# Attention, expert layers and cosine layer on one core: another start for head 0's scores

## The chip, the core and the metric

The kernel runs on one core of a Trainium2 chip. The metric is the device time of one execution in microseconds (us). The kernel before took 740.85 us, the median of three runs (740.27 to 741.19). The profile was taken from one execution of its own, which took 739.14 us; the program's span in that trace is 737.6 us.

The names used here: PE is TensorE (matmuls and transposes), ACT is ScalarE, DVE is VectorE, POOL is GpSimd, SP is SyncE, which issues nearly all DMAs. SBUF is the working memory, PSUM the eight banks into which PE writes.

## The reference

Three layers in a row. Only the first is touched by the change:

```python
q_pool = q.reshape(B, H, S // 2, 2, D).mean(axis=3)      # B=2, H=8, S=1152, D=64
scores = scale * np.matmul(q_pool, k.transpose(0, 1, 3, 2))
attn = softmax(scores)
x = np.matmul(attn, v)          # -> 1152 tokens of 512 columns
x = moe(x)                      # 8 experts, the 2 best of each token
out = (h * np.cos(h)) @ w_out   # h = x @ w_in
```

Neighbouring rows of q are averaged, so each head and batch has 576 pooled rows against 1152 keys.

## The kernel before, in words

Every fp32 operand of a matmul is split in two: a high part, rounded to the format that PE reads (fp32r), and a low part, the rest. A score is q times k in three or four such products. For scores, high and low part of k stand on top of each other in one tile: head_dim is 64, so 64 partitions hold the high part and 64 the low part (`kt`), and the high part of q stands twice (`q2`). One matmul with `q2` then gives high times high plus high times low; a second with the low part of q (`l2`) adds the rest.

Heads go in pairs (hp = 0 to 3), and in a pair there are head hl = 0 and hl = 1. Of each head there are nine tiles of 128 query rows: tiles 0 to 3 lie in batch 0, tile 4 lies in both, tiles 5 to 8 in batch 1. That makes 72 steps, one a tile, and each engine's instructions stand in the order in which the program is written. Step n does, in this order on PE: the scores of tile n+1 (three parts of 384 keys, `s_bank`, L310), between the second and the third of them the first of three groups of transposes of tile n's exponentials (`t_pe`, L348), then the other two groups, and among these 6 or 9 matmuls of attention times v of earlier tiles (L386). DVE takes the maximum of each score part (L324, L326). ACT copies the transposes out (L361, L369), and it does three exponentials with their sums (`s_exp`, L333). POOL splits every third transposed group (L371, L372) and, as single long pieces, v, k and q of heads to come.

PSUM: scores take turns in four banks (`s`), transposes in three (`pt`), attention times v has one (`pa`). A new tile takes the bank that was released longest ago, and PE waits until its last reader is done. With four banks and three score parts a step, the first part of a step's scores needs the exponential of a step earlier, the second part that of part 0 of the tile before, the third that of part 1.

Before the first step stands a prologue (L774 to L862). There head pair 0 is loaded and prepared: q of both heads in two halves (batch 0 first, L206), k of batch 0 in six small pieces (L108), k of batch 1 (L102). DVE adds the q pairs (L211), PE transposes q (`q_front`, L219) and k of both heads together (`k_direct`, L189; ACT L194 takes the high part out of PSUM, DVE L195 the low part), and tile 0's scores start. The rest of pair 0 (batch 1 of q; k of batch 1: `k_group` L180, split on POOL, `k_split`) is prepared between tile 0 and the first steps, with copies on DVE (L845, L847) and ACT (L849) in steps 1 and 2. Ten bf16 matmuls that compute nothing (`warm`, L419) keep PE busy until q is there. A table (`plan`) says in which step the loads, splits and transposes of later heads come.

Of the kernel before, what the change touches and what calls it, by code (L numbers as in the profile page):

```python
# [22 lines left out]
def attn_moe_cos_kernel(ctx, tc, q, k, v, w_gate, w_noise, noise, w1, w2, w_in, w_out, out):  # L23
# [159 lines left out]
    KW = (12, 3, 3, 3)  # L183
    WQ = 10

    def k_direct(hp, b, j, kk, bank):
        p = bank()
        for i in range(3):
            nc.tensor.transpose(p[:, i * 128:(i + 1) * 128], KN[hp, b][:, 3 * j + i].rearrange("p h d -> p (h d)"), ident)  # L189
        cs = slice(384 * j, 384 * (j + 1))  # L190
        for hl, t in enumerate(kk):
            me, ot = slice(hl * 64, hl * 64 + 64), slice(64 - hl * 64, 128 - hl * 64)
            yield
            nc.scalar.activation(t[me, cs], p[me, 0:384], AF.Copy)  # L194
# [20 lines left out]
    def q_front(j, b):  # L215
        QB[j] = p = tbank()
        rs = slice(b * 64, b * 64 + 64)
        for i in range(3):
            nc.tensor.transpose(p[:, i * 64:(i + 1) * 64], QP[0][rs, 3 * j + i].rearrange("p h d -> p (h d)"), ident[rs, rs])  # L219

    def q_part(t, b, j):
        return t[:, b * QB1:b * QB1 + SQ].rearrange("p (s c) -> p s c", c=9)[:, :, 3 * j:3 * j + 3]

    def q_hi(b, j, o):
        nc.scalar.activation(q_part(o, b, j), QB[j][:, 0:192].rearrange("p (i s) -> p s i", i=3), AF.Copy, scale=1.0 / 16.0)

    def q_lo(b, j):
        nc.vector.scalar_tensor_tensor(q_part(QL[0], b, j), QB[j][:, 0:192].rearrange("p (i s) -> p s i", i=3), 1.0 / 16.0,
                                       q_part(QS[0].bitcast(F32), b, j), op0=OP.mult, op1=OP.subtract)
# [498 lines left out]
    def plan():  # L728
# [5 lines left out]
        for hp in range(HP):  # L734
            n0 = 18 * hp
            for hl in range(2):
                for b in range(B):
                    s = n0 + 9 * hl + 5 * b
                    at(s - 7, load_v, hp, hl, b)
                    at(s - 3, split_v, hp, hl, b)  # L740
            if hp:
# [7 lines left out]
                at(m + 2, load_k, hp, 0)  # L749
                for j in range(3):  # L750
                    at(m + (3 + 2 * d, 5 + d, 6 + d)[j], q_group, hp, j)
# [13 lines left out]
                at(n0 + 1, q_bd, hp, 1)  # L765
        at(8, load_gate)
# [4 lines left out]
    pres = ExitStack()  # L771
    pro = pres.enter_context(tc.tile_pool(name="pro", bufs=1, side="right", reuse_waits="tile"))
    load_qb(0, 0)
    load_qb(1, 0)  # L774
    load_k(0, 0)
    load_k(0, 1, pro)
    load_qb(0, 1)
    load_qb(1, 1)
    warm(tbank, WQ)
    QP[0] = prep.tile([128, 9, 2, 64], F32, name="qp", bufs=1)  # L780
    QH = QS[0] = prep.tile([128, 1216], F32R, name="sh", bufs=2)
    QL[0] = prep.tile([128, 1216], F32R, name="ql", bufs=1)
    t = t0 = Q2[0, 0] = qk.tile([128, 1216], F32R, name="q2", bufs=3)
    L0 = QL2[0, 0] = qk.tile([128, 1216], F32R, name="l2", bufs=2)
    for i in range(3):
        z = slice(512 * i, min(512 * i + 512, 1216))
        nc.gpsimd.tensor_scalar(L0[64:128, z], ZERO[64:128, 0:z.stop - z.start], 1.0, 0.0, op0=OP.mult, op1=OP.add)
    for hl in range(2):
        pool_qb(hl, 0, nc.vector)
    for j in range(3):  # L790
        q_front(j, 0)
    kk = k_tiles(0, 0)
    kbank = [lambda: ps.tile([128, 512], F32, name="s", bufs=4)] * 2 + [lambda: ps.tile([128, 512], F32, name="pa", bufs=1)]
    kg = [k_direct(0, 0, j, kk, kbank[j]) for j in range(3)]
    for g in kg:
        next(g)
    for j in range(3):
        q_hi(0, j, QH)
        q_lo(0, j)
    c = slice(0, SQ)  # L800
    nc.scalar.activation(t[64:128, c], QH[0:64, c], AF.Copy)
    nc.vector.tensor_scalar(t[0:64, c], QH[0:64, c], 1.0, 0.0, op0=OP.mult, op1=OP.add)
    nc.gpsimd.tensor_scalar(L0[0:64, c], QL[0].bitcast(F32)[0:64, c], 1.0, 0.0, op0=OP.mult, op1=OP.add)
    for g in kg:
        next(g)
    next(kg[0])
    s_mm(0)
    QR = pro.tile([128, 1216], F32, name="qr")
    z = slice(SQ, QB1)
    nc.gpsimd.memset(QR[:, z], 0.0)  # L810
    nc.gpsimd.tensor_scalar(QH[:, z], QR[:, z], 1.0, 0.0, op0=OP.mult, op1=OP.add)
    for hl in range(2):
        pool_qb(hl, 1, nc.gpsimd)
    QN.clear()
# [4 lines left out]
    load_q(1, 0)  # L819
    load_q(1, 1)  # L820
    for i in range(3):
        s_max(0, i)
    for g in kg[1:]:
        next(g)
    KN.pop((0, 0))
    for j in range(3):
        k_group(0, 1, j)
# [3 lines left out]
    for i in range(3):  # L831
        s_bank(1, i)
        if i == 0:
            for j in range(3):
                q_front(j, 1)
    for i in range(3):
        s_max(1, i)
    for j in range(3):
        q_hi(1, j, QR)
        q_hi(1, j, QH)  # L840
    k_split(0, 1)
    c = slice(SQ, 1216)
    nc.gpsimd.tensor_tensor(QL[0][:, c], QR[:, c], QH.bitcast(F32)[:, c], op=OP.subtract)
    lo0 = QL[0].bitcast(F32)
    ev.setdefault(1, []).insert(0, (lambda: nc.vector.tensor_scalar(  # L845
        t0[0:64, c], QH[0:64, c], 1.0, 0.0, op0=OP.mult, op1=OP.add), ()))
    ev.setdefault(2, []).insert(0, (lambda: nc.vector.tensor_scalar(  # L847
        L0[0:64, c], lo0[0:64, c], 1.0, 0.0, op0=OP.mult, op1=OP.add), ()))
    ev.setdefault(2, []).insert(0, (lambda: nc.scalar.activation(t0[64:128, c], QH[0:64, c], AF.Copy), ()))  # L849
    k_asm_a(0, 1)  # L850
    q_asm(0, 1, False)
    l_asm(0, 1)
    for n in sorted(e for e in ev if e < 0):
        for f, a in ev[n]:
            if f != load_v:
                f(*a)
    pres.close()
    kbp.append(qes.enter_context(tc.tile_pool(name="kbp", bufs=1, reuse_waits="tile")))
    k_stack(0)
    k_asm_b(0, 1)  # L860
    nc.sync.dma_start(KB[0, 1].bitcast(F32)[0:64], KT[0, 1, 0].bitcast(F32)[64:128])
    q_bd(0, 1)  # L862
# [17 lines left out]
    for n in range(NTOT - 1):  # L880
        hp, hl, t = tiles[n]
        for f, a in ev.get(n, []):
            if f not in (q_group, k_group):
# [44 lines left out]
        t_lo(n, 1)  # L928
        if xg:
# [12 lines left out]
        fl = [(f, a) for f, a in ev.get(n, []) if f in (q_group, k_group)]  # L942
# [770 lines left out]
```

## Time and profile before

| what | value |
|---|---|
| median of three runs | 740.85 us (740.27 to 741.19) |
| the profiled execution | 739.14 us |
| its span | 737.6 us |
| PE busy | 722.5 us, 98% of the span |
| DVE, ACT, POOL busy | 562.3, 528.8, 301.9 us |
| PE on the chain that ended last | 90% |

The page's table of 40 slices shows each slice of 18.4 us in tenths of busy time: PE reads 6 in the first slice, 9 in all others but the last. PEclk is the granted TensorE clock in tenths of full speed.

A row of the timeline reads: start in us, duration in us, engine, line of the kernel, operation, out<-in, partitions x elements and type, how many instructions are merged (x3), and in brackets the engine's idle time ahead of it and what ended it. A duration of merged rows is that of the whole group. Instructions of one engine overlap a little, so three in a row take less than three times one.

### The profile page before, as it was taken

How to read it: one execution, taken by the hardware profiler on the slowest of the kernel's cores; microseconds unless marked ns; L12 is line 12 of the kernel's file. 1: busy time of each engine (PE TensorE's matmuls, PEld its weight loads, DVE VectorE, ACT ScalarE, POOL GpSimd, SP SyncE). 2: the span in 40 equal slices, each digit the busy share in tenths (PEclk: the TensorE clock that was granted, in tenths of full speed). 3: DMA queues.
4: the chain of work that ended last, by engine and by line, in shares of the span. 5: the costliest groups of instructions: out<-in, count | busy, mean ns of one | idle time of the engine just before them, and what ended most of it. 6: DMA issues, size and time to landing. Idle time of an engine off the chain costs nothing.

```text
span 737.6 us, 13760 instructions
## 1 busy us (share of the span) xinstructions
PE 722.5 (98%) x4803; PEld 673.9 (91%) x4803; DVE 562.3 (76%) x1161; ACT 528.8 (72%) x1200; POOL 301.9 (41%) x329
## 2 busy tenths in 40 slices
PE   6999999999999999999999999999999999999997
PEld 4899999999999989999999999999889989888885
DVE  5888788888878988879889887776677776556562
ACT  5999799979988964458777676766588665555443
POOL 5988867877977973212022021103187110000000
PEclk9999999999999999999999999999999999999999
DMA  9957756695665511798999999968353210010001
GB/s 207 244 94 183 184 130 147 163 237 106 161 140 146 179 44 29 248 314 295 363 371 328 334 345 330 329 233 286 119 171 97 85 29 1 1 44 0 1 1 60
DMA packets 75329, 125.02 MB, mean 169 GB/s; under 512 B 11950, under 2 KB 42030, under 8 KB 75254
## 3 DMA queue, kind: packets, MB, share of 16 engines
q1 hardware_dynamic: 68678, 101.92, 47.3%
q0 software_dynamic: 5568, 19.14, 7.4%
q10 hardware_dynamic: 1008, 3.02, 1.6%
q8 instruction: 40, 0.66, 0.4%
q14 instruction: 35, 0.29, 0.1%
HBM read 82.15 MB, written 20.33 MB: 139 GB/s over the span
## 4 chain that ended last, share of the span: by engine, by line
PE 90%; DVE 4%; ACT 3%; DMA 1%; issue 0%; SPq 0%; ACTq 0%; DVEq 0%
PE h L1145 20%; PE acc L1145 16%; PE acc L1177 11%; PE s L310 10%; PE pa L386 9%; PE pt L348 9%; PE t L1145 7%; PE pt L694 2%; PE t L1137 1%; PE pt L984 1%; PE t L1194 1%; PE pt L180 1%; DMA raw<-in_moe_w_dram 1%; DVE nm L324 1%; DVE el L365 1%; DMA qn<-in_q_dram 1%
## 5 line engine op out<-in xcount | busy, mean ns | idle before, releaser
L324 DVE TENSOR_REDUCE nm<-s 128x1 f32<-128x384 f32 x216 | 112.1, 551 | 23.4 <-PE s L310 21.8
L333 ACT ACTIVATE p<-s,nm 128x384 f32<-128x384 f32 x216 | 125.1, 583 | 2.8 <-DVE nm L326 1.5
L1145 PE MATMUL h<-xe,u 128*128 128x320 f32 (+5 forms) x768 | 120.1, 306 | 0.0
L1145 PEld LDWEIGHTS h<-xe,u 128*128 128x128 f32 x768 | 109.6, 188 | 0.5
L642 DVE TENSOR_TENSOR u<-raw,u 128x1024 fp32r<-128x1024 f32 x66 | 80.9, 1227 | 34.4 <-ACT u L641 33.6
L348 PE MATMUL pt<-ident,p 128*128 128x128 f32 x645 | 105.0, 272 | 0.0
L310 PE MATMUL s<-kt,q 128*128 128x384 f32 x240 | 88.8, 386 | 3.7 <-DVE kt L195 2.1
L348 PEld LDWEIGHTS pt<-ident,p 128*128 128x128 f32 x645 | 81.7, 140 | 5.7
L386 PE MATMUL pa<-eh,v 128*128 128x320 f32 (+1 forms) x279 | 86.5, 324 | 0.0
L641 ACT ACTIVATE u<-raw 128x1024 fp32r<-128x1024 f32 x73 | 77.1, 1057 | 10.3 <-DMA raw<-in_moe_w_dram 5.8
L361 ACT ACTIVATE eh<-pt 128x384 fp32r<-128x384 f32 x144 | 68.9, 501 | 20.3 <-PE pt L348 19.0
L386 PE MATMUL pa<-el,v 128*128 128x320 f32 (+1 forms) x279 | 82.4, 309 | 0.0
L372 POOL TENSOR_TENSOR el<-rw,eh 128x384 fp32r<-128x384 f32 x71 | 71.9, 1012 | 5.9
L365 DVE TENSOR_TENSOR el<-pt,eh 128x384 fp32r<-128x384 f32 x144 | 72.9, 547 | 1.0 <-ACT eh L361 0.9
L1177 PE MATMUL acc<-hh,u 128*128 128x320 f32 (+5 forms) x448 | 71.8, 302 | 0.1
L1145 PE MATMUL acc<-u,gh 128*128 128x512 f32 x216 | 66.9, 391 | 0.0
L310 PE MATMUL s<-kt,l 128*128 128x384 f32 x198 | 66.3, 337 | 0.0
L1177 PEld LDWEIGHTS acc<-hh,u 128*128 128x128 f32 x448 | 64.7, 188 | 0.4 <-ACT hh L1156 0.4
L1232 POOL DMA_DIRECT2D w_d<-dw x16 | 9.0, 563 | 130.5 <-DVE dw L1231 130.5
L371 POOL TENSOR_SCALAR eh<-rw 128x384 fp32r<-128x384 f32 x71 | 36.8, 518 | 42.0 <-ACT rw L369 39.7
L386 PEld LDWEIGHTS pa<-el,v 128*128 128x128 f32 x279 | 52.9, 190 | 0.0
L386 PEld LDWEIGHTS pa<-eh,v 128*128 128x128 f32 x279 | 52.8, 189 | 0.0
(292 smaller groups left out, 1605.9 us busy)
## 6 DMA issues: line engine op xcount, KB each, us to landing
raw<-in_moe_w_dram SPq DMA_DIRECT2D x64, 512.0 KB
raw<-in_moe_w_in_dram SPq DMA_DIRECT2D x16, 512.0 KB
raw<-in_moe_w_out_dram SPq DMA_DIRECT2D x16, 512.0 KB
w_d<-dw POOLq DMA_DIRECT2D x16, 512.0 KB, 5.4
raw<-w_d SPq DMA_DIRECT2D x13, 512.0 KB
vn<-in_v_dram SPq DMA_DIRECT2D x16, 288.0 KB
q<-sh SPq DMA_DIRECT2D x14, 304.0 KB
l<-ql SPq DMA_DIRECT2D x14, 304.0 KB
```

Source lines behind the costliest of these rows:

```text
L310: nc.tensor.matmul(o, l, r, start=(m == 0), stop=(m == len(mm) - 1))
L324: nc.vector.tensor_reduce(NM[n][:, i:i + 1], SB[n][i][:, 0:384], axis=AX.X, op=OP.max, negate=True)
L333: nc.scalar.activation(P[n][i], SB[n][i][:, 0:384], AF.Exp, bias=NM[n][:, 3:4], accum_out=SUMS[:, t, 2 * hp + hl, i:i + 1])
L348: nc.tensor.transpose(p[:, c], P[n][j][:, c], ident)
L361: nc.scalar.activation(t_dst(n, j)[0], t_src(n, j), AF.Copy)
L365: nc.vector.tensor_tensor(el, t_src(n, j), ef, op=OP.subtract)
L372: nc.gpsimd.tensor_tensor(el, rw, ef, op=OP.subtract)
L386: nc.tensor.matmul(st["p"][:, 0:w], V2[hp, hl, b][:, VC[c] if hp + b else c, :], (EH, EL)[s][:, c, EB[g]:EB[g] + w], start=(c == 0 and s = ...
L641: nc.scalar.activation(b[:, 0], r, AF.Copy)
L642: st_w["lo"].tensor_tensor(b[:, 1], r, b.bitcast(F32)[:, 0], op=OP.subtract)
L1145: nc.tensor.matmul(o, l, r, start=first and i == 0, stop=last and i == len(seq) - 1)
L1177: nc.tensor.matmul(ACC[e, d][:, 0:CAPS[e]], w[:, i, 128 * d:128 * d + 128], r[:, 0:CAPS[e]], start=f == 0 and r is hh and i == 0, stop=f = ...
```

## The change

Only the start is changed, and the handling of head pair 0.

- Loads: q and k of head 0 alone, batch 0 first, in four whole DMAs (`load_h0`); then two loads of v, then q of head 1 (`load_h1`). k of head 1 (`load_k1`) follows once head 0's k has been transposed.
- q of head 0: DVE adds the pairs in two pieces (6 and 3 of 9 groups, `pool_p`), ACT writes each sum a second time beside it, so that one transpose gives both copies of q. ACT takes the high part and DVE the low part out of PSUM straight into `q2` and `l2` (`q0_hi`, `q0_lo`). Batch 1 is added on POOL and goes the same way after tile 0's maxima.
- k of head 0: batch 0 is transposed alone (`k0_tr`, 64 columns each) and split by ACT and DVE (`k0_part`); batch 1 by `k0b_copy` (three copies on ACT) and `k0b_split` (POOL and four DMAs).
- Head 1 is prepared inside the steps: its k in steps 1 to 3 (`k_group`, 3 transposes and one ACT copy each, split on POOL in step 4, eight DMAs in step 6), its q in steps 4 to 6 (`q1_group`: 3 transposes, two ACT copies; the low parts on DVE a step later, `late`). These groups take their PSUM bank from the four of the scores (`gbank`).
- One q group of head pair 1 moves from step 6 to step 7, one split of v from step 2 to step 5, one load of k from step 2 to step 4. The idle matmuls are eleven and read a tile of ones, which is set first on DVE.

```diff
@@ functions of the prologue @@
+    XS0 = X.rearrange("p t d -> p (t d)")[:, 1920:1920 + S]
     def k_group(hp, b, j):
...
-        p = tbank()
+        p = tbank() if hp else gbank()
...
+    PART = (slice(0, 6), slice(6, 9))
+    def pool_p(hl, rs, cs, eng):
+        t = QN[0, hl][rs].rearrange("p (s r) d -> p s r d", r=2)
+        o = QP[0, hl][rs, cs]
+        eng.tensor_tensor(o[:, :, 0, :], t[:, cs, 0, :], t[:, cs, 1, :], op=OP.add)
+        if eng is nc.vector:
+            nc.scalar.activation(o[:, :, 1, :], o[:, :, 0, :], AF.Copy)
+        else:
+            eng.tensor_scalar(o[:, :, 1, :], o[:, :, 0, :], 1.0, 0.0, op0=OP.mult, op1=OP.add)
+    def gbank():
+        return ps.tile([128, 512], F32, name="s", bufs=4)
...
+    def q1_group(j):
+        cs = slice(3 * j, 3 * j + 3)
+        q_tr(1, slice(0, 128), cs, ("h", j))
+        src = QB["h", j][:, 0:384].rearrange("p (i b s) -> p b s i", i=3, b=2)
+        for b in range(2):
+            nc.scalar.activation(q0_out(Q2[0, 1], b, cs), src[:, b], AF.Copy, scale=1.0 / 16.0)
+        late.append(lambda: [nc.vector.scalar_tensor_tensor(q0_out(QL2[0, 1], b, cs), src[:, b], 1.0 / 16.0,
...
+    def k0_tr(j, p):
         for i in range(3):
...
+            nc.tensor.transpose(p[LO, i * 128:(i + 1) * 128], KN[0, 0][:, 0, c:c + 64], ident)
+    def k0_part(j, p):
+        kt, c = KT[0, 0, 0], slice(384 * j, 384 * j + 384)
+        nc.scalar.activation(kt[LO, c], p[LO, 0:384], AF.Copy)
+        nc.vector.tensor_tensor(kt[HI, c], p[LO, 0:384], kt.bitcast(F32)[LO, c], op=OP.subtract)
+    def k0b_copy():
...
+        k_tr(1, 0, pa)
+        nc.scalar.activation(t[:, 0:384], pa[:, 0:384], AF.Copy)
+        k_tr(1, 1, pb)
+        nc.scalar.activation(t[:, 384:512], pb[:, 0:128], AF.Copy)
+        nc.scalar.activation(t[LO, 512:640], pb[LO, 128:256], AF.Copy)
...
@@ plan @@
-                    at(m + (3 + 2 * d, 5 + d, 6 + d)[j], q_group, hp, j)
+                    at(m + (3 + 2 * d, 5 + 2 * d, 6 + d)[j], q_group, hp, j)
...
+        for j in range(3):
+            at(1 + j, k_group, 0, 1, j)
+            at((4, 5, 6)[j], q1_group, j)
+        at(4, k_split, 0, 1)
+        at(6, k1_asm)
@@ the prologue @@
+    for i in range(2):
+        pool_p(0, LO, PART[i], nc.vector)
+        q_tr(0, LO, PART[i], (0, i))
...
+    for i in range(2):
+        q0_hi(0, i)
+        q0_lo(0, i)
+    for j in range(3):
+        k0_part(j, kb3[j])
+    pool_p(0, HI, slice(0, 9), nc.gpsimd)
     s_mm(0)
...
     for i in range(3):
         s_max(0, i)
+    for i in range(2):
+        q_tr(0, HI, PART[i], (1, i))
+        q0_hi(1, i)
+        q0_lo(1, i)
+    k0b_copy()
+    load_k1()
+    k0b_split()
     for i in range(3):
         s_exp(0, i)
```

ACT from its first copy to tile 0's three exponentials, before (`sh`, `ql`: high and low part of q; `st`: k of batch 1):

```order
L225 ACTIVATE sh<-pt 128x64x3 x3
L801 ACTIVATE q_170<-sh 64x576
L194 ACTIVATE kt<-s 64x384 x2
L194 ACTIVATE kt<-pa 64x384
L194 ACTIVATE kt<-s 64x384 x2
L194 ACTIVATE kt<-pa 64x384
L181 ACTIVATE st<-pt 128x384 x3
L333 ACTIVATE p,SUMS<-s,nm 128x384 x3
```

The same stretch of ACT now (`qp`: the pooled q, `X`: scratch for k of batch 1):

```order
L216 ACTIVATE qp<-qp 64x6x64
L216 ACTIVATE qp<-qp 64x3x64
L241 ACTIVATE q_168<-pt 128x64x6
L241 ACTIVATE q_168<-pt 128x64x3
L284 ACTIVATE kt<-s 64x384 x2
L284 ACTIVATE kt<-pa 64x384
L241 ACTIVATE q_168<-pt 128x64x6
L241 ACTIVATE q_168<-pt 128x64x3
L292 ACTIVATE X<-pt 128x384
L294 ACTIVATE X<-pt 128x128
L295 ACTIVATE X<-pt 64x128
L432 ACTIVATE p,SUMS<-s,nm 128x384 x3
```

Head 1's key parts and the copy of q have gone from here, the two second copies of the sums stand in front, and the q and k of batch 1 now stand ahead of the exponentials.

PE from the third score part of tile 3 (step 2) to the first of tile 4 (step 3), before:

```order
L310 MATMUL s<-kt,q_170 128x384
L310 MATMUL s<-kt,l_171 128x384
L348 MATMUL pt<-ident,p 128x128 x3
L386 MATMUL pa<-eh,v_323 128x256
L386 MATMUL pa<-el,v_323 128x256
L386 MATMUL pa<-eh,v_323 128x256
L386 MATMUL pa<-el,v_323 128x256
L348 MATMUL pt<-ident,p 128x128 x3
L386 MATMUL pa<-eh,v_323 128x256
L386 MATMUL pa<-el,v_323 128x256
L310 MATMUL s<-kt,q_170 128x384 x2
```

The same stretch of PE now:

```order
L409 MATMUL s<-kt,q_168 128x384
L409 MATMUL s<-kt,l_169 128x384
L447 MATMUL pt<-ident,p 128x128 x3
L485 MATMUL pa<-eh,v_221 128x256
L485 MATMUL pa<-el,v_221 128x256
L485 MATMUL pa<-eh,v_221 128x256
L485 MATMUL pa<-el,v_221 128x256
L447 MATMUL pt<-ident,p 128x128 x3
L485 MATMUL pa<-eh,v_221 128x256
L485 MATMUL pa<-el,v_221 128x256
L182 MATMUL s<-ident,kn 128x128 x3
L409 MATMUL s<-kt,q_168 128x384 x2
```

One row is new, L182: three transposes of head 1's k at the end of the step, into a bank of the scores. Steps 1 to 3 have it, and steps 4 to 6 have one with q of head 1. So four tiles a step take turns in the four banks. Behind the first four of these groups (steps 2 to 5) each score part takes the bank of the same part of the tile before, and the third score part stands on PE ahead of the matmuls with v.

## Rows read from the trace of the kernel before

**Rows 1.** The page: busy time by engine, granted clock in 40 slices.

```profile
PE 722.5 (98%) x4803; PEld 673.9 (91%) x4803; DVE 562.3 (76%) x1161; ACT 528.8 (72%) x1200; POOL 301.9 (41%) x329
PEclk9999999999999999999999999999999999999999
```

**Rows 2.** Busy time by stretch: PE, PEld, DVE, ACT, POOL, clock, DMA share, GB/s.

```profile
30.00:35.00 5.00, 5.00 (x38) 4.69 (x38) 4.81 (x12) 5.00 (x17) 4.75 (x7) 1.00 1.07 240
```

**Rows 3.** Timeline of the prologue, from the first load to the first exponential.

```profile
4.90 0.75 DVE L211 TENSOR_TENSOR qp<-qn 64x576 f32<-64x576 f32 x1 [2.32 <-DMA qn<-in_q_dram]
...
6.41 0.75 DVE L211 TENSOR_TENSOR qp<-qn 64x576 f32<-64x576 f32 x1 [0.76 <-DMA qn<-in_q_dram]
...
7.31 0.74 PE L219 MATMUL pt<-ident,qp 64*128 64x64 f32 x9 [0.64 <-DVE qp L211]
7.71 0.82 ACT L225 ACTIVATE sh<-pt 128x192 fp32r<-128x192 f32 x3 [5.45 <-PE pt L219]
...
8.57 0.68 ACT L801 ACTIVATE q<-sh 64x576 fp32r<-64x576 f32 x1
...
9.08 0.81 POOL L803 TENSOR_SCALAR l<-ql 64x576 fp32r<-64x576 f32 x1 [4.39 <-DVE ql L228]
9.27 0.86 ACT L194 ACTIVATE kt<-s 64x384 fp32r<-64x384 f32 x2
9.79 1.01 DVE L195 TENSOR_TENSOR kt<-s,kt 64x384 fp32r<-64x384 f32 x2 [0.44 <-ACT kt L194]
...
10.39 0.44 PE L310 MATMUL s<-kt,q 128*128 128x384 f32 x1 [0.91 <-DVE kt L195]
...
11.92 0.44 PE L310 MATMUL s<-kt,q 128*128 128x384 f32 x1 [0.43 <-DVE kt L195]
...
12.13 2.78 POOL L211 TENSOR_TENSOR qp<-qn 64x576 f32<-64x576 f32 x2 [1.83 <-DMA qn<-in_q_dram]
...
13.41 0.16 DVE L326 TENSOR_REDUCE nm<-nm 128x1 f32<-128x3 f32 x1
...
14.03 0.60 ACT L333 ACTIVATE p<-s,nm 128x384 f32<-128x384 f32 x1
```

**Rows 4.** Timeline of steps 0 and 1: score parts, an exponential, two copies on DVE.

```profile
17.81 0.63 ACT L333 ACTIVATE p<-s,nm 128x384 f32<-128x384 f32 x1
...
18.56 0.67 DVE L845 TENSOR_SCALAR q<-sh 64x640 fp32r<-64x640 f32 x1
18.58 0.44 PE L310 MATMUL s<-kt,q 128*128 128x384 f32 x1 [0.40 <-ACT p L333]
...
19.28 0.42 PE L310 MATMUL s<-kt,q 128*128 128x384 f32 x1
...
21.66 1.48 DVE L847 TENSOR_SCALAR l<-ql 64x640 fp32r<-64x640 f32 x1
```

**Rows 5.** Timeline of steps 3 to 6: third score parts (PE), first and third exponentials (ACT).

```profile
26.60 0.60 PE L310 MATMUL s<-kt,q 128*128 128x384 f32 x2
...
28.43 0.58 ACT L333 ACTIVATE p<-s,nm 128x384 f32<-128x384 f32 x1
...
29.86 0.42 PE L310 MATMUL s<-kt,q 128*128 128x384 f32 x1
...
29.93 0.59 ACT L333 ACTIVATE p<-s,nm 128x384 f32<-128x384 f32 x1
...
31.33 0.58 ACT L333 ACTIVATE p<-s,nm 128x384 f32<-128x384 f32 x1
...
32.76 0.42 PE L310 MATMUL s<-kt,q 128*128 128x384 f32 x1
...
36.44 0.42 PE L310 MATMUL s<-kt,q 128*128 128x384 f32 x1
```

**Rows 6.** Timeline of PE at the end of step 6: a group of three transposes.

```profile
38.86 0.49 PE L136 MATMUL pt<-ident,qp 128*128 128x128 f32 x3
39.11 0.42 PE L310 MATMUL s<-kt,q 128*128 128x384 f32 x1
```

More of the change, by code (lines that the diff above doesn't have):

```diff
@@ L213, in attn_moe_cos_kernel @@
-    QB = {}
[L215 to L225, printed above, removed]
@@ L227, in q_lo, with load_h0 @@
-    def q_lo(b, j):
-        nc.vector.scalar_tensor_tensor(q_part(QL[0], b, j), QB[j][:, 0:192].rearrange("p (i s) -> p s i", i=3), 1.0 / 16.0,
-                                       q_part(QS[0].bitcast(F32), b, j), op0=OP.mult, op1=OP.subtract)
+    WQ = 11
+    XF = X.rearrange("p t d -> p (t d)")
+    VC0 = tuple(range(9))
+    def load_h0(eng, kind, b):
+        if kind == "q":
+            if b == 0:
+                QN[0, 0] = prep.tile([128, 18, 64], F32, name="qn", bufs=2)
+            eng.dma_start(QN[0, 0][b * 64:(b + 1) * 64], q[b, 0].rearrange("(p r) d -> p r d", r=18))
+        else:
+            if b == 0:
+                KN[0, 0] = prep.tile([128, 2, 576], F32, name="kn", bufs=1)
+            eng.dma_start(KN[0, 0][:, b], k[b, 0].rearrange("(p c) d -> p (c d)", c=9))
@@ new lines, in attn_moe_cos_kernel, with q_tr, q_hi, q0_out @@
+    QB = {}
+    def gbank():
+        return ps.tile([128, 512], F32, name="s", bufs=4)
+    def q_tr(hl, rs, cs, key):
+        w = rs.stop - rs.start
+        QB[key] = p = gbank() if hl else tbank()
+        for i in range(cs.stop - cs.start):
+            nc.tensor.transpose(p[:, i * w:(i + 1) * w], QP[0, hl][rs, cs.start + i].rearrange("p k d -> p (k d)"), ident[rs, rs])
+    def q_hi(key, o, n):
+        nc.scalar.activation(o, QB[key][:, 0:n], AF.Copy, scale=1.0 / 16.0)
+    def q0_out(t, b, cs):
+        return t[:, b * QB1:b * QB1 + SQ].rearrange("p (s c) -> p s c", c=9)[:, :, cs]
@@ new lines, in attn_moe_cos_kernel, with gap, q1_open, k_tr @@
+    late = []
+    def gap(t):
+        nc.gpsimd.tensor_scalar(t[:, SQ:QB1], ZERO[:, 0:QB1 - SQ], 1.0, 0.0, op0=OP.mult, op1=OP.add)
+    def q1_open():
+        Q2[0, 1] = qk.tile([128, 1216], F32R, name="q2", bufs=3)
+        QL2[0, 1] = qk.tile([128, 1216], F32R, name="l2", bufs=2)
+        gap(Q2[0, 1])
+        gap(QL2[0, 1])
+    def k_tr(b, i, p):
+        kn = KN[0, 0][:, b]
+        for m in range(3 if i == 0 else 2):
+            c = 384 * i + 128 * m
+            w = min(128, 576 - c)
+            nc.tensor.transpose(p[0:w, 128 * m:128 * m + 128], kn[:, c:c + w], ident)
@@ new lines, in k0b_split, with k1_asm @@
+    def k0b_split():
+        r = KS.pop((0, 0))
+        h = prep.tile([128, 1216], F32R, name="sh", bufs=2)[:, 0:640]
+        nc.gpsimd.tensor_scalar(h, r, 1.0, 0.0, op0=OP.mult, op1=OP.add)
+        nc.gpsimd.tensor_tensor(r, r, h.bitcast(F32), op=OP.subtract)
+        KT[0, 0, 1] = qk.tile([128, S], F32R, name="kt", bufs=5)
+        k_put(KT[0, 0, 1][LO], h.bitcast(F32), 0)
+        k_put(KT[0, 0, 1][HI], r, 0)
+    def k1_asm():
+        h, r = KS.pop((0, 1))
+        K1H.append(h)
+        for b in range(2):
+            KT[0, 1, b] = qk.tile([128, S], F32R, name="kt", bufs=5)
+        for b in range(2):
+            k_put(KT[0, 1, b][HI], r, b)
+        for b in range(2):
+            k_put(KT[0, 1, b][LO], h.bitcast(F32), b)
@@ L231, in k_split, with k1_bd, k1_open @@
+    def k1_bd():
+        h = K1H[0]
+        for b in range(2):
+            k_put(KB[0, 1][b * 64:b * 64 + 64], h.bitcast(F32), b)
+            c0 = 4 * 128 if b == 0 else 4 * 128 - SQ + QB1
+            nc.sync.dma_start(QD[0, 1].bitcast(F32)[b * 64:b * 64 + 64],
+                              QL2[0, 1].bitcast(F32)[b * 64:b * 64 + 64, c0:c0 + 128])
+    K1H = []
+    def k1_open():
+        QD[0, 1] = kbp[0].tile([128, 128], F32R, name="qd", bufs=2)
     def k_split(hp, b):
@@ L770, in attn_moe_cos_kernel @@
     ev = plan()
[L771 to L778, printed above, removed]
-    warm(tbank, WQ)
[L780 to L814, printed above, removed]
+    kbp.append(qes.enter_context(tc.tile_pool(name="kbp", bufs=1, reuse_waits="tile")))
+    k_stack(0)
+    load_h0(nc.sync, "q", 0)
+    load_h0(nc.sync, "k", 0)
+    load_h0(nc.sync, "q", 1)
+    load_h0(nc.sync, "k", 1)
+    warm(tbank, WQ)
+    QP[0, 0] = prep.tile([128, 9, 2, 64], F32, name="qp", bufs=1)
+    QP[0, 1] = XF[:, 128:1280].rearrange("p (c k d) -> p c k d", c=9, k=2)
     for n in sorted(e for e in ev if e < 0):
@@ L818, in attn_moe_cos_kernel @@
                 f(*a)
-    load_q(1, 0)
-    load_q(1, 1)
+    load_h1()
+    t0 = Q2[0, 0] = qk.tile([128, 1216], F32R, name="q2", bufs=3)
+    L0 = QL2[0, 0] = qk.tile([128, 1216], F32R, name="l2", bufs=2)
+    KT[0, 0, 0] = qk.tile([128, S], F32R, name="kt", bufs=5)
+    gap(t0)
+    gap(L0)
+    for i in range(2):
+        pool_p(0, LO, PART[i], nc.vector)
+        q_tr(0, LO, PART[i], (0, i))
+    kb3 = [ps.tile([128, 512], F32, name="s", bufs=4) for _ in range(2)]
+    kb3.append(ps.tile([128, 512], F32, name="pa", bufs=1))
+    for j in range(3):
+        k0_tr(j, kb3[j])
+    for i in range(2):
+        q0_hi(0, i)
+        q0_lo(0, i)
+    for j in range(3):
+        k0_part(j, kb3[j])
+    pool_p(0, HI, slice(0, 9), nc.gpsimd)
+    s_mm(0)
+    for n in sorted(e for e in ev if e < 0):
+        for f, a in ev[n]:
+            if f != load_v:
+                f(*a)
     for i in range(3):
         s_max(0, i)
[L823 to L827, printed above, removed]
+    for i in range(2):
[5 more added lines that the diff above has]
+    k0b_split()
     for i in range(3):
@@ L832, in attn_moe_cos_kernel, with pool_h1 @@
         s_bank(1, i)
-        if i == 0:
-            for j in range(3):
-                q_front(j, 1)
     for i in range(3):
         s_max(1, i)
[L838 to L862, printed above, removed]
+    def pool_h1():
+        pool_p(1, slice(0, 128), slice(0, 9), nc.gpsimd)
+        QN.pop((0, 1))
+        load_q(1, 1)
+        q1_open()
+    QN.pop((0, 0))
+    load_q(1, 0)
+    ev.setdefault(1, []).insert(0, (pool_h1, ()))
     NPOP = (9, 9, 6, 6, 6, 9, 9, 9, 9)
@@ L928, in attn_moe_cos_kernel @@
         t_lo(n, 1)
+        if late:
+            late.pop(0)()
         if xg:
```

66 lines of the change are left out of this document (34 added, 32 removed).

## The prediction

> **What bounds the kernel now.** I read the page first: PE is busy for 722.5 of 737.6 us, and its granted clock is full (2.4 GHz) in all 40 slices [rows 1]. So time is won or lost only where PE does not run through, or where its work changes. The windows say where that is: from 30 to 35 us PE is busy for 5.00 of 5.00 us, and ACT too [rows 2]. What the change does to the end is therefore what it does to PE's place in the program some 40 us in; everything behind is the same work, and I count it through 1:1. Then I read the timeline of the prologue and the steps.
>
> The chain at the start runs: the second q load lands, 6.41; transposes, 7.31; high part on ACT, 7.71; k high and low parts, 9.27 and 9.79; first score, 10.39; third score, 11.92; tile 0's maxima done, 13.57; first exponential, 14.03 [rows 3]. In the steps I follow one mark: the start on PE of the third score part of a tile. It stands at 19.28 for tile 2, 26.60 for tile 4, 29.86, 32.76 and 36.44 for tiles 5 to 7 [rows 4, 5].
>
> **The start, gained.** The first load is unchanged and lands at 4.9; the old chain waited for the second, 1.5 later [rows 3]. The transfers are of one size and come in order, so I let the next ones land 1.5 apart as well: k at 6.4, second q at 7.9.
>
> - DVE adds 64x384 where 64x576 took 0.75: about 0.55, to 5.45. ACT's second copy of it: 64x576 took 0.68, so 0.5, to 5.95. The pieces of 192 run beside these.
> - PE: 0.15 from an operand to the first transpose, as 7.16 to 7.31. Three transposes later ACT started, 0.40 on; six take 0.60. ACT starts its high part at 6.7. The two parts cost 0.45 and 0.27 (three of 192 columns took 0.82), to 7.4. k has landed and is transposed by 7.9.
> - ACT takes k's high parts at 0.4 each (two took 0.86) from 7.4. DVE does two low parts of q to 8.0, then k's low parts, 0.55 for the first and 0.47 for each further one (two took 1.01): 8.55, 9.0, 9.5.
> - So tile 0's first score starts at 8.6 where it was 10.39, and the third at 9.55 where it was 11.92. The maxima end 1.65 behind the third start, as now (11.92 to 13.57): 11.2. That is 2.4 early [all from rows 3].
>
> **The start, given back.** ACT now has batch 1 ahead of tile 0's exponentials: two q parts and three k copies, where the three k copies of before stood; PE has their transposes ahead of tile 1's scores. They need POOL's pooled sum: landed 7.9, 1.39 for the addition (two took 2.78), 0.81 for the second copy (as L803): 10.1 [rows 3]. Then six transposes, ACT at 10.8, 0.72 for the q parts, 0.5 for the first k copy, to 12.05. The last two transposes of k take the bank that this copy reads, so PE waits for it: 0.45, then two small copies, 0.4: the first exponential at 12.95, against 14.03 [rows 3]. Of 2.4 us 1.1 are left.
>
> Part of this comes back, as the six q copies of before (0.82 for three) and the later copies of batch 1 go (L845, L847 on DVE, L849 on ACT). Three exponentials to 14.65, at 0.57 each, a short wait and two copies of transposes to 15.95, the first exponential of tile 1, against 17.81. The second score part of tile 2 starts 0.77 behind it, and the third 0.70 later, as now (17.81, 18.58, 19.28): 17.4, against 19.28 [rows 4]. The lead is 1.9 us.
>
> L845 and L847 are the same copy: 0.67, and 1.48 where POOL was at work too [rows 4]. The Trainium skill (GPSIMD Engine Reference, 8. Key points) says why: POOL shares its SBUF interfaces with VectorE, and they collide where DVE runs a two-port mode or has two SBUF inputs. These rows agree. By that rule POOL's sum of batch 1 stays at its 1.39, since DVE's work beside it reads PSUM with one SBUF input; were the rule wider than that, rival B's price would be due.
>
> **The steps, lost.** In the steps of the first four new groups (tiles 3 to 6) the third score part needs the third exponential of the tile before, where it needed the second. That closes a ring, which the trace prices in three intervals: third score part to first exponential, 1.47 (29.86 to 31.33); first to third exponential, 1.50 (28.43 to 29.93) [rows 5]; start of an exponential to the matmul that needs its bank, 0.77 [rows 4]. Together 3.74 a step, and 0.36 more for tile 4, which has twice the matmuls (26.60 to 28.43 is 1.83, not 1.47) [rows 5]. From 17.4 the mark is at 21.15, 24.9, 29.0 and 32.75 for tiles 3 to 6; now tile 6 is at 32.76 [rows 5]. The lead is gone: steps that took 2.90 (29.86 to 32.76) take 3.74.
>
> The Trainium skill (Perfetto Trace Analysis, Optimizing Tensor Performance) asks for independent matmul groups to rotate through different PSUM banks, so that the reading of one overlaps the next. It speaks against this change, which puts a fourth user into a ring of four. The row agrees: PE idle 0.40 us until an exponential had freed a bank [rows 4]. With the ring the sum is this one; without it, rival A's.
>
> **Extra PE work.** From tile 6 on PE is full again, and groups count. One costs 0.25 (38.86 to 39.11), and 0.08 more for the first matmul behind it: 0.33 [rows 6]. Step 5 has one more (36.44 - 32.76 + 0.33 = 4.0, above the ring's 3.74), step 6 as many as before, as one q group left it, step 7 one more. The ring of step 6 has ACT 0.05 late at most. That is 0.66, and the lead was 0.0. ACT copies of head 1 (0.4 to 0.45 each) lie in the 1.4 us between the third exponential of one tile and the first of the next; DVE's low parts stand behind its own step's work, which is shorter than PE's 3.7 to 4.0.
>
> At nothing I count: the eleven idle matmuls (they start earlier and end by 5.9, when no operand is there yet; if they ran 0.5 longer, the whole start would slip by that), the four DMAs of head 0's k of batch 1 (by these sums ready near 18, needed at 23), head 1's eight (33 to 40, needed at 43), and POOL, whose pieces are those of before in another order. Without that cover each microsecond late there is one at the end.
>
> **Sum.** -1.9 (lead at tile 2) + 1.9 (four steps) + 0.66 = about 0.6 us slower: 739.14 becomes 739.8, and the median of 740.85, which lies 1.7 above this execution, 741.4.
>
> **Rivals.**
>
> A. The ring does not decide; ACT does. For it: ACT is full in the windows, and its step is 2.90 (28.43 to 31.33); with a copy of 0.4 it is 3.3 [rows 2, 5]. Four steps at 3.3, not 3.74 (and 3.3 for tile 4 too), give back 0.44 x 4 + 0.36 = 2.1: 739.3, 0.2% faster. Against it: the bank order is written in the program, and a wait of that kind is in the rows already.
>
> B. Slower: POOL's sum of batch 1 comes late. It stands on PE ahead of k's transposes and of tile 1's scores, and on ACT ahead of all exponentials, so from 10.0 on each microsecond goes to the end. In the rows the same halves landed only at 12.13 (as loads 9 and 10) [rows 3]. One transfer later than I think (9.4) costs 1.5: 742.9. If POOL is slowed as L847 was (1.48 for 0.67), 2.2 becomes 4.9, and the time 744.1. Against it: third in the queue, nothing is ahead of it but two equal loads.
>
> C. The change doesn't do what it says: k of batch 0 lands not second, at 6.4, but two transfers later, at 9.4 by the same spacing. Then k's transposes end at 10.6, three us later than above, and the first score stands at about 10.9, no earlier than now. The 1.9 are not won: 743.3.
>
> **From these to the numbers.** The forecast 0.58, A 0.24, B 0.13, C 0.05. What a measurement tells from no change here is 0.2%, 1.5 us: below 739.4 is faster, above 742.3 slower. A lies on the lower bound, and with half of its chance under it, and a start somewhat earlier than mine, faster is 0.16. B and C and the upper end of the forecast (each of some thirty durations is good to 0.05) make 0.22 slower. The rest, 0.62, is the same. The forecast alone ranges from 740.2 to 742.3; with A, and with the near half of B, 739.1 to 743.0.
>
> **What would show it.** The first score near 8.6, tile 0's maxima done near 11.2, its first exponential near 13; tile 2's mark near 17.4. Then PE idle before the score parts of tiles 3 to 6, released by ACT's exponentials, at 3.7 us a step, and the mark of tile 6 where it is now. Marks of tiles 3 to 6 3.3 apart would be A; PE or ACT waiting for POOL's sum, B; the first transposes of k waiting for a DMA, C. I am wrong altogether if PE's marks behind step 8 differ from now by over 1.5 us, or if the end differs by something that isn't there at 50 us.

## The result and the profile after

The change made the kernel slower, and by more than the range allowed: 744.67 us (median of six, 742.66 to 745.01) against 740.68 (six runs of the kernel before, 738.61 to 741.36), a ratio of 1.0059 with a 95% interval of 1.0041 to 1.0077. Forecast were 741.4, 739.1 to 743.0. The profiled execution took 744.77 us, its span 743.1; against the profile before that is 5.63 more.

The page of the kernel after answers to [rows 1]:

```profile
PE 727.9 (98%) x4818; PEld 677.7 (91%) x4818; DVE 561.8 (76%) x1162; ACT 528.6 (71%) x1201; POOL 302.0 (41%) x331
```

PE is 5.4 us longer busy for fifteen instructions more. Part of it are matmuls that ran longer (at full clock the same instructions take 726.0, in the first experiment below). The windows of PE say where: us from to, length, PE busy, granted clock, DMA share, GB/s.

```profile
8.00:11.00 3.00, 3.00 (x13) 0.50 1.07 287
...
58.00:60.00 2.00, 1.06 (x7) 1.00 0.67 145
60.00:62.00 2.00, 1.01 (x6) 1.00 0.80 170
62.00:63.00 1.00, 1.00 (x7) 0.65 0.91 180
63.00:64.00 1.00, 1.00 (x6) 0.50 0.94 178
...
65.00:66.00 1.00, 1.00 (x7) 0.65 1.02 396
```

There are two stretches at 1.2 GHz (clock 0.50): one in the prologue, and one at 62 to 66 us, with PE half idle from 58 to 62 just ahead of it. The first is at the start that the change was about. Its timeline (DVE, PE, ACT) answers to [rows 3]:

```profile
5.80 0.82 DVE L214 TENSOR_TENSOR qp<-qn 64x384 f32<-64x384 f32 x2 [3.23 <-DMA qn<-in_q_dram]
...
7.05 0.74 PE L229 MATMUL pt<-ident,qp 64*128 64x64 f32 x9 [1.76 <-ACT qp L216]
7.72 1.49 PE L280 MATMUL s<-ident,kn 128*64 128x128 f32 x6
...
9.73 0.69 PE L409 MATMUL s<-kt,q 128*128 128x384 f32 x1
...
14.23 0.57 ACT L432 ACTIVATE p<-s,nm 128x384 f32<-128x384 f32 x1
```

The first addition, which waits for the first q load, started at 5.80, not at 4.90 as before; PE idled 1.76 us, its clock fell, and six k transposes took 1.49 us, where the same six took 0.85 at full clock in another run (last section). The second place is tile 13, the one tile of head 1 with queries of both batches. Its low parts come from two tiles of their own, `kb` and `qd`. PE there, in the kernel after and then before:

```profile
58.49 0.59 PE L409 MATMUL s<-kt,q 128*128 128x384 f32 x2
60.99 0.44 PE L409 MATMUL s<-kb,qd 128*128 128x384 f32 x1 [1.91 <-DMA qd<-l]
...
65.51 0.43 PE L409 MATMUL s<-kt,q 128*128 128x384 f32 x1
```

```profile
56.33 0.59 PE L310 MATMUL s<-kt,q 128*128 128x384 f32 x2
56.77 0.34 PE L310 MATMUL s<-kb,qd 128*128 128x384 f32 x1
...
59.69 0.33 PE L310 MATMUL s<-kt,q 128*128 128x384 f32 x1
```

From tile 13's first part to tile 14's, 3.36 us have become 7.02: PE waits 1.91 for a DMA, and runs at half clock behind that. Why that DMA came so late, SP's rows of the kernel after tell, with one of POOL behind them:

```profile
41.05 0.68 SPq L81 DMA_DIRECT2D GW<-in_moe_w_gate_dram  x1
...
51.17 1.11 SPq L164 DMA_DIRECT2D l<-ql  x2
52.32 2.78 SPq L172 DMA_DIRECT2D qd<-ql  x2
55.15 1.24 SPq L348 DMA_DIRECT2D kb<-sh  x2
56.49 0.54 SPq L322 DMA_DIRECT2D qd<-l  x1
57.07 1.74 SPq L348 DMA_DIRECT2D kb<-sh  x2
58.91 0.54 SPq L322 DMA_DIRECT2D qd<-l  x1
```

```profile
48.34 2.81 POOL L149 TENSOR_TENSOR ql<-st,sh 128x1216 fp32r<-128x1216 f32 x1
```

In the kernel before the same pieces stand in the prologue of the program, and SP had issued the last of them by 32 us:

```profile
28.57 1.18 SPq L249 DMA_DIRECT2D kb<-sh  x2
29.80 0.59 SPq L861 DMA_DIRECT2D kb<-kt  x1
30.59 1.41 SPq L172 DMA_DIRECT2D qd<-ql  x2
```

The change has a function that the prediction never priced, `k1_bd`: four DMAs for `kb` and two for `qd`, set in the plan at step 9. There they stand on SP behind the pieces of head pair 1, whose low part `ql` POOL finishes only at 51.15 us (48.34 + 2.81). That wait is only the start of it: SP then issues ten DMAs one after the other, four of head pair 1 (51.17 to 55.10) and these six (55.15 to 59.45). The last of the six left at 58.91 and landed at 60.95; PE had been idle since 59.08.

The difference is 2.16 us at tile 10's third score part (49.35 against 47.19) and 5.82 at tile 14's first (65.51 against 59.69). From there to the end the two traces stay 5.1 to 5.8 us apart.

### The profile page after: what moved, and what is told of

Its sections match the earlier page's. It is cut to its first block, busy times and chain, and to the rows that moved or that the text cites. A ratio compares the mean times of both kernels' runs of the same rounds, so it can differ in the third digit from the quotient of the medians.

```text
span 743.1 us, 13782 instructions
## 1 busy us (share of the span) xinstructions
PE 727.9 (98%) x4818; PEld 677.7 (91%) x4818; DVE 561.8 (76%) x1162; ACT 528.6 (71%) x1201; POOL 302.0 (41%) x331
## 4 chain that ended last, share of the span: by engine, by line
PE 88%; DVE 3%; ACT 3%; DMA 2%; POOL 2%; issue 1%; SPq 0%; ACTq 0%; POOLq 0%; DVEq 0%
PE h L1224 20%; PE acc L1224 14%; PE acc L1256 13%; PE s L409 10%; PE pa L485 8%; PE pt L447 8%; PE t L1224 7%; PE pt L793 1%; PE t L1273 1%; PE t L1216 1%; PE pt L1063 1%; DMA raw<-w_d 1%; DVE nm L423 1%; DMA qn<-in_q_dram 1%; ACT p L432 1%
```

## The experiments

Each was timed beside the kernel before on one chip; the ratio is to that kernel. A mark is the start of a tile's third score part, as in the prediction. Theory: the late pieces cost the time. Rival: the start and the steps account for it, and the wait at tile 13 only stands in for another.

**The pieces early.**

```diff
-        at(9, k1_open)
-        at(9, k1_bd)
+        at(8, k1_open)
+        at(8, k1_bd)
         at(8, load_gate)
```

> The changed kernel with head 1's block-diagonal KB and QD pieces issued at the head of step 8 instead of the end of step 9. Theory (late pieces): the 1.91 us wait for QD at tile 13 and the half-speed stretch behind it go, tile 14's first score part comes 2.2 us behind the kernel before instead of 5.8, and the time is 744.7 - 3.7 = 741.0. Rival (the start and the steps account for the loss, and the wait at tile 13 only takes the place of another one there): PE waits at tile 13 for something else, and the time stays within 1 us of 744.7.

740.56 us, ratio 1.0006 (0.9995 to 1.0018). The wait and the half clock behind it are gone, the step has its 3.36 us again:

```profile
57.87 0.34 PE L409 MATMUL s<-kb,qd 128*128 128x384 f32 x1
...
60.80 0.34 PE L409 MATMUL s<-kt,q 128*128 128x384 f32 x1
```

Some 4 us of the loss were these six DMAs; what is left, 0.5, can't be told from none. Tile 14 is 1.1 behind the kernel before, not 2.2: in this execution the first addition started at 5.23, not 5.80, and the clock did not fall in the prologue.

**The late pieces alone, in the kernel before.** `late_bd` copies `kb` and `qd` at step 9, behind head pair 1's pieces, in six DMAs where the prologue had five; nothing else is changed.

```diff
+        at(9, late_bd)
```

> The kernel before, with only head 1's KB and QD pieces moved from the prologue to the end of step 9, behind head pair 1's low part and its QD. Theory (late pieces): PE waits at tile 13 for QD, some 1.5 to 2 us, the granted clock falls behind it, and the time is 740.4 + 3.7 = 744. Rival (the changed start and steps are needed for the loss): no wait of PE at tile 13, and 740.4 within 0.5.

741.57 us, ratio 1.0033 (1.0011 to 1.0054). The wait is there, without the changed start:

```profile
58.52 0.41 PE L320 MATMUL s<-kb,qd 128*128 128x384 f32 x1 [1.54 <-DMA qd<-l]
...
61.51 0.34 PE L320 MATMUL s<-kt,q 128*128 128x384 f32 x1
```

So the pieces are enough for a loss. It is smaller than expected: the wait is 0.4 shorter, and in this execution the clock did not fall behind it (1.00 in every window from 60 to 68 us), so the step costs 1.77 more, not 3.66. Three of the twelve times lie at 743.1 to 748.1, at a mean clock of 0.993 to 0.997; whether the clock fell at tile 13 in those is not on record.

**The same kernel again.**

> The changed kernel, unchanged, beside the others on one chip. All theories: 744.7. If the wait costs 1.9 us always and the clock behind it only in some executions, its times fall into two groups, one near 742.5 with a mean granted clock of 0.998 or more and one near 744.7 or above with 0.994 to 0.996; if the cost is one, they form one group.

744.24 us, ratio 1.0065 (1.0048 to 1.0082): one group, 742.87 to 745.60, all at a mean clock of 0.995 to 0.997. In both profiles of the kernel after, the clock falls behind this wait. Of the other executions only the mean clock is on record, and it is low in all of them (0.994 to 0.997; 0.996 to 1.000 with the pieces early). In this profile the first load landed at 4.79, and the clock stayed full in the prologue:

```profile
4.79 0.82 DVE L214 TENSOR_TENSOR qp<-qn 64x384 f32<-64x384 f32 x2 [2.21 <-DMA qn<-in_q_dram]
...
8.66 0.44 PE L409 MATMUL s<-kt,q 128*128 128x384 f32 x1 [0.77 <-DVE kt L285]
...
59.86 0.69 PE L409 MATMUL s<-kb,qd 128*128 128x384 f32 x1 [2.22 <-DMA qd<-l]
```

**Further back, and only half of it early.** In the one `k1_bd` goes to step 10, in the other the `qd` pieces go to step 8 and the `kb` pieces stay at step 9.

```diff
-        at(9, k1_bd)
+        at(10, k1_bd)
```

> The changed kernel with the KB and QD pieces one place further back on SP, at step 10, behind the two q pieces of head pair 1's second head (1.24 us on the queue). Theory (the queue position sets the wait): PE waits 1.2 us longer at tile 13, 3.1 us in all, and the time is 744.7 + 1.2 = 745.9 or, with the clock lower for longer, up to 746.5. Rival (the wait is set by something other than SP's order): 744.7 within 0.4.

```diff
-        at(9, k1_bd)
+        at(8, k1_bd, (1,))    # qd alone
+        at(9, k1_bd, (0,))    # kb alone
```

> The changed kernel with the two QD pieces at step 8 and the four KB pieces left at the end of step 9. Theory (any of the six pieces behind the low part of head pair 1 is late): the last KB piece now lands about 0.6 us earlier than QD did, so PE still waits at tile 13, for KB, some 1.3 us, and the time is 742.5 to 744. Rival (only QD, the last of the six, is late): no wait at tile 13, and 740.6 as in e1_bd_early.

The first: 747.03 us, ratio 1.0094 (1.0076 to 1.0112), a wait of 4.68 us where 3.1 was expected:

```profile
62.74 0.66 PE L409 MATMUL s<-kb,qd 128*128 128x384 f32 x1 [4.68 <-DMA qd<-l]
```

SP took 3.00 us for its first two `kb` pieces, against 1.24 in the kernel after; why is not known. More delay, more wait: the theory's direction. The second: 746.01, ratio 1.0085 (1.0068 to 1.0101), worse than the change itself; neither theory had that. Its SP rows and PE's wait:

```profile
44.64 1.10 SPq L324 DMA_DIRECT2D qd<-l  x2
45.79 1.41 SPq L81 DMA_DIRECT2D GW<-in_moe_w_gate_dram  x1
...
58.89 3.35 SPq L350 DMA_DIRECT2D kb<-sh  x4
```

```profile
63.70 0.69 PE L411 MATMUL s<-kb,qd 128*128 128x384 f32 x1 [4.57 <-DMA kb<-sh]
```

`qd` needs DVE's last low part of head 1, so SP stood still until 44.64, and the eight gate loads behind it began at 45.79 where they had begun at 41.05. All that follows moved back, `kb` too; here POOL's low part was done before SP came to it (51.1 against 53.2 us), and SP's own queue is the delay. The edit that has all six early pays the same delay, but there only the gate loads and pieces of head pair 1 stand behind it, and PE waits for none of them. The Trainium skill (DMA: Bandwidth & Descriptors, Anatomy of one DMA, on DMAs issued from gpsimd) puts a DMA's wait on the issuing sequencer, ahead of dispatch. SP's rows agree, as these eight loads need nothing of `qd`.

**The wait filled.** Nine idle matmuls ahead of tile 13's score, the pieces late as in the change.

```diff
+        if (n, i) == (13, 0):
+            warm(lambda: SB[n][i], 9)
```

> The changed kernel with nine idle matmuls of 128x512 (about 1.9 us at full clock) on PE at tile 13, ahead of its score, into the bank that the score then overwrites; the late pieces are as in the changed kernel. Theory (the wait costs twice, once as idle time and once as the clock behind it): PE no longer idles there, the granted clock stays 1.00 from 60 to 66 us, tile 14 comes 1.75 us earlier than in the changed kernel, and the time is 744.7 - 1.75 = 742.9. Rival (the wait alone costs, the clock falls anyway): 744.7 or more.

742.57 us, ratio 1.0038 (1.0022 to 1.0053): 1.7 to 2.1 below the two medians of the change, where 1.75 was expected; the intervals still overlap. Of the wait 0.79 was left in the profiled execution, and the clock stayed 1.00 from 60 to 66 us:

```profile
57.79 2.11 PE L520 MATMUL s<-ONES 128*128 128x512 bf16 x9
...
61.03 0.44 PE L409 MATMUL s<-kb,qd 128*128 128x384 f32 x1 [0.79 <-DMA qd<-l]
...
64.06 0.34 PE L409 MATMUL s<-kt,q 128*128 128x384 f32 x1
```

From the score that waited to tile 14's first it is 3.03 us here, and 4.52 in both traces without the idle matmuls (60.99 to 65.51 in the kernel after): 1.49 of the 1.75 are seen. The whole step took 6.27 us from the first idle matmul, against 7.02 and 7.34, as the pieces landed later in it. (That execution is the longest of nine, 746.72. Up to 341 us it is level with the trace of the same kernel again; at 353 PE waits 1.77 us for DVE and then runs at 1.2 GHz, and from there it is 3.0 us behind. Waits of 0.6 to 1.6 us at that place stand in three traces that have the pieces early too.) What the step from tile 13 to 14 costs, from the rows of each trace:

| kernel | wait for the DMA | step | step - 3.36 - wait |
|---|---|---|---|
| before | 0 | 3.36 | 0 |
| pieces early | 0 | 3.36 | 0 |
| before, pieces late | 1.54 | 5.13 | 0.23, clock not fallen |
| after | 1.91 | 7.02 | 1.75 |
| after again | 2.22 | 7.34 | 1.76 |
| `qd` alone early | 4.57 | 10.42 | 2.49 |
| one place further back | 4.68 | 10.38 | 2.34 |

Where the clock fell, the last column is what the half clock behind the wait takes: 1.75 behind waits of 1.91 and 2.22, and 2.3 to 2.5 behind waits of 4.6.

**The start: the order of the loads, and more idle matmuls.** Both on top of the pieces early; the first has both q loads ahead of both k loads, the second fifteen idle matmuls instead of eleven.

> As e1_bd_early, with head 0's two q loads issued before the two k loads. Theory (k's packets share the queue with the first q): the first pooled sum starts at 4.9 again instead of 5.8, but k lands later; where k is not the later one, the first score comes 0.9 us earlier and the time is 0.5 to 0.9 below that of e1_bd_early. Rival (k then lands after the transposes of q are done, and the first score waits for it): first k transposes at 8 or later, no gain, or a loss of up to 0.5.

> As e1_bd_early, with fifteen idle matmuls at the start instead of eleven, so that PE is busy to about 6.8 us, where the first q transposes come at 7.05. Theory (PE's 1.76 us of idling before them made the granted clock fall to 0.50): the clock stays 1.00 from 8 to 11 us, six k transposes take 0.87 us instead of 1.49, the third score starts near 10.3 instead of 11.14, and the time falls by 0.3 to 0.8 us below e1_bd_early's. Rival (the idle matmuls do not hold the clock, or POOL's sum of batch 1 at 10.15 takes the gain): clock 0.5 there as before, or the clock is up and the mark of tile 2 stays at 18.7; the same time within 0.2.

Loads: 740.30 us, ratio 1.0006 (0.9995 to 1.0016). The first add starts at 4.85 and the first score at 8.71, against 5.23 and 9.10; k is not late. The 0.4 us won is less than the time can tell. Matmuls: 741.39, ratio 1.0012 (0.9999 to 1.0025), no gain. The clock was full from 5 to 11, but so it was with eleven, so the theory had nothing to win here. In this execution the clock fell a little later, behind PE's waits of 0.77, 0.58 and 0.73 us:

```profile
13.00:14.00 1.00, 0.27 (x2) 1.00 0.39 41
14.00:15.00 1.00, 1.00 (x4) 0.59 0.80 260
```

**The steps: who holds the scores' ring.** All with the pieces early. The first edit puts head 1's three k groups into the transposes' ring:

```diff
-        p = tbank() if hp else gbank()
+        p = tbank()
```

> As e1_bd_early, with the three transposed groups of head 1's keys (steps 1 to 3) in the transposes' ring of three banks instead of the scores' ring of four. Theory (the closed ring sets the pace of those steps): the marks of tiles 3 to 5 come closer by about 0.3 us each, and the time falls by about 1 us below e1_bd_early's. Rival (ACT or PE sets the pace, not the ring): marks as before, the same time within 0.3; or the three banks of the transposes now hold PE up, and it is slower by up to 1 us.

739.95 us, ratio 0.9994 (0.9982 to 1.0005): 0.6 below the kernel with the pieces early, where about 1 was expected, and not told apart from it. Marks from tile 2 to 6 lie 3.25, 4.00, 3.64 and 3.72 apart, where the kernel with the pieces early has 3.71, 3.96, 4.05 and 3.73: two of three steps are 0.4 shorter, the one with twice the matmuls (to tile 4) is not (the fourth step has a q group, still in the scores' ring). With the q loads first as well:

> Three edits on the changed kernel: the KB and QD pieces at step 8, both q loads ahead of both k loads, the transposed groups of head 1's keys in the transposes' ring. Theory (the edits add up: -0.2 and -0.6 beside the one that has the pieces early): 739.7, and the marks of tiles 3 to 6 about 0.9 us ahead of e3_qq_kk's. Rival (what is won in the steps waits at a later place): the marks are ahead by less than 0.4 and the time is that of the kernel before, 740.1.

739.90 us, ratio 1.0000 (0.9988 to 1.0013), the marks as expected (tile 6 at 31.89 against 32.75), but tile 10 stands at 47.12: level with the kernel before (47.19), and so is the time. Then head 1's q groups too, their low parts on DVE at once instead of a step later:

> As c1_early_qqkk_ktbank, with head 1's three transposed q groups (steps 4 to 6) in the transposes' ring as well, their low parts on DVE in the same step. Theory (no step has a fourth user of the scores' ring now, and steps 4 to 6 run at PE's pace): the mark of tile 7 another 0.5 to 0.8 us earlier, 739.1. Rival (DVE's low parts now stand ahead of the next tile's maxima and hold up its exponentials): the marks of tiles 5 to 7 as in c1 or later, 739.7 or more.

743.53 us, ratio 1.0044 (1.0029 to 1.0059); the rival, far stronger than thought. ACT waits for a tile's maxima, and DVE's low part ahead of those had waited for ACT:

```profile
34.74 0.58 ACT L432 ACTIVATE p<-s,nm 128x384 f32<-128x384 f32 x1 [1.64 <-DVE nm L425]
```

```profile
32.40 0.67 DVE L254 SCALAR_TENSOR_TENSOR l<-pt,q 128x192 fp32r<-128x192 f32 x2 [1.53 <-ACT q L252]
32.95 1.50 DVE L423 TENSOR_REDUCE nm<-s 128x1 f32<-128x384 f32 x3
```

Three steps of 5.4, 5.1 and 5.4 us follow. The step of the first q group itself, ahead of these, became 0.4 shorter (3.31 against 3.71). The `late` list of the change keeps the low parts out of this loop.

**A version that beats both.** The theory here is that the lead at the start goes into six groups of head 1 in full steps. On top of the version that was level, three of them go to places where PE idles, with their k loaded early:

```diff
     for i in range(3):
         s_bank(1, i)
+        if i == 0:
+            k1_tr(0)      # three transposes; the same in steps 1 and 2
     for i in range(3):
         s_max(1, i)
+        if i == 0:
+            k1_copy(0)    # on DVE, not on ACT
```

> On top of c1_early_qqkk_ktbank: head 1's k loads are issued right behind head 0's, into a stretch of X of their own, and its three transposed groups stand behind the first score part of tiles 1, 2 and 3, where PE idles 0.73, 0.51 and 0.60 us for ACT or for a bank, their copies on DVE behind that tile's first maximum. Theory (the change lost its lead because six groups of head 1 went from PE's idle time in the prologue into full steps, at 0.33 us each): three of them are free again, the mark of tile 10 comes 47.12 - 1.0 = 46.1, and the time is 739.0, 0.15% below the kernel before. Rival (DVE's copies hold up the maxima of tiles 1 to 3, or the earlier k loads delay head 1's q): the mark of tile 10 at 47.1 or later, 740 or more.

738.83 us, ratio 0.9985 (0.9972 to 0.9998): faster than before, by little. The first group fits into the wait for ACT, of which 0.40 is left:

```profile
12.55 0.49 PE L282 MATMUL pt<-ident,X 128*128 128x128 f32 x3
13.44 0.44 PE L421 MATMUL s<-kt,q 128*128 128x384 f32 x1 [0.40 <-ACT p L444]
```

Tile 10's mark is at 45.76, 1.43 ahead of the kernel before; expected was 46.1. The gain, 1.26 of it, lies in the three steps from tile 2 to 5, where the edit is, and it is more than the three groups at 0.33 each. The edit also takes three copies from ACT to DVE, so what the transposes gave and what the copies gave is not told apart.

## Why the prediction was wrong

| third score part, us | tile 2 | tile 6 | tile 9 | tile 10 |
|---|---|---|---|---|
| before | 19.28 | 32.76 | 43.83 | 47.19 |
| predicted | 17.4 | 32.75 | 44.5 (+0.66) | 47.8 (+0.6) |
| after | 18.67 | 34.15 | 45.99 | 49.35 |
| after again | 17.21 | 32.67 | 44.53 | 47.89 |

- **The failed step: "At nothing I count ... head 1's eight (33 to 40, needed at 43)".** Head 1 has fourteen DMAs in the steps, not eight. The other six, `kb` and `qd` at step 9, were never looked at, nor their place on SP behind a low part that POOL ends at 51. The sentence "everything behind is the same work, and I count it through 1:1" hid it. Their price is 3.7 to 4.0 us in two traces (1.9 to 2.2 of wait, 1.75 of half clock), and about 4 in the medians with them late and early. With that price the forecast of 741.4 would have been some 745.3. The half clock was not in the sum at all: the prediction took the clock as full everywhere, as the profile of the kernel before shows it. Without the late pieces the kernel takes 740.56, inside the range, and 0.5 above the kernel before, where 0.6 was forecast.
- **The prediction's own test for this** held: the end differs (5.63 us) by something that is not there at 50 us (2.16 at tile 10). Its other test, marks behind step 8 that differ by over 1.5 us, is met in the first trace (2.16) and not in the second (0.70).
- **First load at 4.9: right in one execution, 0.9 off in another.** It was taken over from a kernel with another load behind it. Where it did land at 4.79, the first score came at 8.66 (8.6 predicted) and the lead at tile 2 was 2.07 (1.9). The maxima were done at 11.24 (11.2) and the first exponential came at 12.77 (12.95). Where it landed at 5.80, PE idled and the clock fell, the first exponential came at 14.23, and the lead was 0.61. Some 1.0 us of that difference is the load and 0.4 the clock: in a run with the first addition at 5.84 and the clock full, tile 2's mark is at 18.26.
- **The steps: right in size, and the ring is there.** From tile 2 to 6 the second trace takes 15.46 us, the first 15.48; predicted 15.35. The three intervals of the ring are in the trace, 1.50, 1.50 and 0.74 where 1.47, 1.50 and 0.77 were priced:

```profile
30.41 0.44 PE L409 MATMUL s<-kt,q 128*128 128x384 f32 x1
...
31.91 0.59 ACT L432 ACTIVATE p<-s,nm 128x384 f32<-128x384 f32 x1
...
33.41 0.59 ACT L432 ACTIVATE p<-s,nm 128x384 f32<-128x384 f32 x1
...
34.15 0.44 PE L409 MATMUL s<-kt,q 128*128 128x384 f32 x1
```

  Three of the four steps keep to it (3.72, 4.05 with the 0.36 of tile 4, and 3.74), and each of these became 0.4 to 0.5 shorter when its group left the scores' ring. The one with twice the matmuls (3.97, to tile 4) does not keep to it, and did not become shorter. The sign named for the ring, PE idle ahead of the score parts, shows at tile 3 alone (0.53 us). Further on PE reads busy: at tile 6 the row of three transposes ahead of the score part starts at 33.66, lasts 0.49 us and ends where the score part starts, while in the kernel before the score part starts 0.25 behind the same row (32.51 and 32.76). Such a wait is seen in the starts of the rows and not as idle time. The Trainium skill (Perfetto Trace Analysis, Optimizing Tensor Performance) asks for banks that rotate, and these steps agree.
- **Extra groups 0.66: 0.77 and 0.79** (tiles 6 to 9: 11.84 and 11.86 against 11.07), mis-sized by little.
- **Rivals.** A is out: the marks are not 3.3 apart. B and C as well: POOL's sum began at 7.99 (7.9 predicted) and took 1.41 and 0.67, and k's transposes wait for no DMA. None of the three, nor the case of slower, had the mechanism that decided.
- **A row misread for rival B.** The prediction sets a copy of 0.67 us (L845) against one of 1.48 "where POOL was at work too". POOL was at work beside the first as well, from 18.84 on, and it still took 0.67. So these two rows do not show what slowed the second.

```profile
18.84 1.81 POOL L843 TENSOR_TENSOR ql<-qr,sh 128x640 fp32r<-128x640 f32 x1
```

## What to carry to other kernels

Go through every DMA that a change moves, on the queue that issues it: what stands ahead there, what that waits for, and when the data is needed. A small piece behind another tile's wait is as late as that wait and the issue of all that stands between, and moving one waiting piece forward delays all behind it. Work moved from an engine's idle time into its full time has to be paid there (two groups of three transposes cost 0.77 us), however short the prologue becomes.

## What the hardware showed

- A wait of PE costs twice where the clock falls behind it: 1.91 and 2.22 us of wait were each followed by a loss of 1.75 at half clock. Idle time alone does not tell whether it falls. In the prologue 1.76 us ahead of the first transposes were followed by half clock, and 1.24 in the kernel with the k groups moved were not (rows below); 1.54 at tile 13 were not. In two traces it fell at 14 us behind waits of under 0.8 us, and the same waits stand in most of the other traces without a fall.

```profile
7.10 0.74 PE L229 MATMUL pt<-ident,qp 64*128 64x64 f32 x9 [1.24 <-ACT qp L216]
7.77 0.85 PE L280 MATMUL s<-ident,kn 128*64 128x128 f32 x6
```

- The first addition, which waits for the first load alone (288 KB), began between 4.79 and 5.84 us in the eight profiles of kernels with k's load second, and between 4.75 and 4.90 in the six with an equal q load second. That k's packets are the cause was not isolated further.
